# Layer one's last pair of blocks: its second product as seven products too, and partial sums copied from bank to bank by ScalarE

## The chip, the cores and the metric

The kernel runs on one core of a Trainium2 chip. The metric is the device time of one execution in microseconds (us), the median of the runs shown. The engines are named as in the profile: PE is TensorE (matmuls) and PEld its weight loads, DVE is VectorE, ACT is ScalarE, SP issues the DMAs (SPq is its queue). ns are nanoseconds.

## What is computed

Attention over chunks, and then two feed-forward layers over 3072 tokens of 512 features, all in float32 (arguments shortened here):

```python
def _moe_ref(x, w_in, w_out, s, b):      # layer one
    h = x @ w_in                         # (3072, 512) @ (512, 2048)
    r = np.maximum(h, 0.0)
    g = s * (r * r) + b
    return (g @ w_out).astype(np.float32)

def _moe2_ref(x, w_in, w_out):           # layer two
    h = x @ w_in
    g = h * (1.0 / (1.0 + np.exp(-1.702 * h)))
    return (g @ w_out).astype(np.float32)

def reference(**kwargs):
    ...
    attn_out = _attn_ref(**attn_kwargs)
    x = np.ascontiguousarray(attn_out.transpose(0, 2, 1, 3)).reshape(B * S, H * D)
    x = _moe_ref(x=x, **moe_kwargs)
    return _moe2_ref(x=x, **moe2_kwargs)
```

## The kernel before, in words

The tokens are cut into 6 blocks of 512. Features lie on the 128 partitions, tokens along the free dimension. A float32 factor is split into a high part that the matmul takes without loss (fp32r) and a low rest, so each product of 128 x 128 weights with 512 columns is three matmuls: high x high, high x low, low x high. An "h" or "l" at the end of a name (wih and wil, xh and xl) says which part it is. The weights arrive as 64-bit floats; `words` turns the two 32-bit halves of each into a float32 (absolute value, clamp, shift, add, sign), and the split follows.

The work runs in five stretches, in the profile's microseconds:

- 0 to 447: attention, and layer one of blocks 0 to 3, one unit after another (`step`; L614 to L616 are the first product, L652 the second).
- 447.8 to 612: layer one of blocks 4 and 5, the last pair (`seven(0)`).
- 612 to 771, 771 to 930 and 930 to the end: layer two, a pair of blocks at a time (`wino(s)`, s = 1, 2, 3).

A pair is multiplied in the way of Strassen and Winograd: weights and inputs are cut into 2 x 2 pieces, sums of pieces are formed, and seven products replace eight. With p counting the eight pairs of hidden tiles, `wino` makes for each p the products A (A11 x B11), B (S2 x T2), C (S3 x T3), A2 (A12 x B21, added into A's bank), D (S1 x T1), C2 (A22 x T4, into C's bank) and D2 (S4 x B22, into D's bank), six matmuls of 512 columns each (L1240 to L1242). The partial sums leave the banks: ScalarE copies A to a spot of the SBUF tile ys (p1, L1277), and VectorE adds a bank to a spot (L1273) for u2 (B), u3 (C), c22 (D), c21 (C2) and c12 (D2). `gates` (L1251) makes G, the hidden values, from A's bank and the spots. When all p are done the second product follows (L1358): sums of G (L1341), their split into oq and oj (L1329 on ScalarE, L1332 on VectorE), and seven products of 96 matmuls with 256 columns.

The last pair is done by functions of its own. Its first product has the same seven products (L1020 to L1022). Its second is the plain one (L1098): 16 hidden tiles, 4 output tiles, 3 terms and 2 blocks, 384 matmuls of 512 columns. The gates of the pair's second block wait in DRAM (gd) in between.

PSUM: A's and C's banks at even p are two single tiles ph; B and D share the tile pb, one half each. At odd p A and C are the halves of one tile, pc, and B and D the halves of another, pd. `space` says so, in both kernels:

```python
if p % 2:
    return ("accA" if c in "AC" else "accB", ("two", s, p, c in "AC"), "ABCD".index(c) // 2)
return ("h", ("h", s, p, c), None) if c in "AC" else ("a", ("two", s, p, False), "BD".index(c))
```

The order on each engine is made by `Plan.order`: every operation has a due number, durations by engine and the operations that it comes after; the plan starts on each engine what can start soonest, among these what is due first. The program is written out in that order, and waits are put in where tiles are shared. Where TensorE would idle early, the plan fills in small matmuls (idle).

Inputs of a pair come through the SBUF tile xf: `fetch(0)` and `fetch(1)` each load half of both blocks, and sums, copies and splits turn them into the operands; xf has two buffers.

Of the kernel before, what the change touches and what calls it, by code (L numbers as in the profile page):

```python
# [40 lines left out]
HELD = 4  # L41
# [7 lines left out]
class Plan:  # L49
# [24 lines left out]
    def order(self):  # L74
# [108 lines left out]
        full, clock = [], 0.0  # L183
        for i, e in chosen:
            if e == "pe":
                idle = min(starts[i], starts[self.first]) - clock
# [8 lines left out]
def attention_moe_moe(ctx: ExitStack, tc: tile.TileContext, q_t, k_w, v_w, w_in1, w_out1, s_b, w_in2, w_out2, out):  # L195
# [22 lines left out]
    wod = [[dram.tile([P, 7, 2, 256], F32, name=f"wod{x}{p}") for x in "hl"] for p in range(NF // 4)]  # L218
    gd = [dram.tile([P, 2, 512], F32, name=f"gd{j}") for j in range(NF)]
# [4 lines left out]
    plan.first = None  # L224
# [87 lines left out]
    def prep(i):  # L312
        m, o, j = w = weights[i]
        need = (at_o if o else at_h)[index[m, j]] - 0.5
        tag = "wo" if o else "wi" if j < NWI else "wj" if j < NWI + NWJ else "wz"
        def tiles(e):
            T[w] = weight_tiles(tag)

        def high(e):
            copy(e, T[w][0], T["u", i].bitcast(F32))  # L320

        def rest(e):
            hi, lo = T[w]
# [3 lines left out]
        d = op(need, {"act": 0.62}, lambda e: (tiles(e), high(e)), after=[d], alloc=[(tag, w)], uses=[("u", i)])  # L327
        f = op(need, {"dve": 0.62}, rest, after=[d], uses=[("u", i)])
        o_w[w] = (d, f)

    def words(i, w, need, late=()):
# [8 lines left out]
        def absolute(e):  # L340
            u = T["u", i] = stp.tile([P, 512], U32, tag="u", name="u", bufs=4)
            hi = T["st", i][:, :, 1]
            if e == "act":
                nc.scalar.activation(out=u.bitcast(F32), in_=hi.bitcast(F32), func=AF.Abs)
            else:
                nc.vector.tensor_single_scalar(out=u, in_=hi, scalar=0x7FFFFFFF, op=ALU.bitwise_and)

        def clamp(e):
            uf = T["u", i].bitcast(F32)
            nc.vector.tensor_scalar(out=uf, in0=uf, scalar1=2.0**-15, scalar2=122880.0, op0=ALU.max, op1=ALU.min)  # L350

        def low(e):
            lo = T["st", i][:, :, 0]
            nc.scalar.activation(out=lo.bitcast(F32), in_=lo, func=AF.Copy, scale=2.0**-51, bias=2.0)  # L354
# [18 lines left out]
        b = op(need, {"act": 0.67} if m == 0 else {"act": 0.67, "dve": 0.36}, absolute, after=[a], alloc=[("u", u)], uses=[st])  # L373
        d = op(need, {"dve": 0.36}, clamp, after=[b], uses=[u])
        d = op(need, {"dve": 0.36}, shift, after=[d], uses=[u])
        d = op(need, {"dve": 0.62}, add, after=[c, d], uses=[u, st])
        return op(need, {"dve": 0.62}, sign, after=[d], uses=[u, st])

# [7 lines left out]
    plan.tag("xf", 2)  # L386
    plan.tag("gq", 2)
    plan.tag("yz", 2)
# [14 lines left out]
    def attend(u):  # L403
# [152 lines left out]
        z = op(pt, {"dve": 0.1 + 0.55 * n}, top, after=s + [z], alloc=[("small", ("top", u))], uses=[("sc", u)])  # L556
# [41 lines left out]
    def step(i):  # L598
        m, b, j, r, v = units[i]
        n = (r.stop - r.start) / 512  # L600
        busy = v < 2
# [68 lines left out]
        if busy:  # L670
            d = op(need, {"act": 0.2 + 0.52 * n}, affine, after=[d], uses=[("r", i)])
        else:
            d = op(need, {"dve": 0.1 + 0.3 * n}, gate2, after=[d], uses=[("r", i)])
        g1 = op(need, {"act": 0.19 + 0.43 * n}, gate3, after=[d], alloc=[("g", ("g", i))], uses=[("r", i)])
        g2 = op(need, {"dve": 0.12 + 0.54 * n}, gate4, after=[g1], uses=[("r", i)])
        for k in range(KT):
# [4 lines left out]
            if plan.first is None:  # L681
                plan.first = d
# [47 lines left out]
    def combine(p):  # L730

        w0, w1 = (0, 0, 2 * p), (0, 0, 2 * p + 1)
        need = at_h[len(units) - 1] + 20

        def keep(v, w, src, dst):
            def fn(e):
                nc.sync.dma_start(out=wc[0][p][v][:, dst], in_=T[w][v].bitcast(F32)[:, src].rearrange("p (n d) -> p n d", d=256))
            return fn

        first = list(o_w[w0]) + list(o_w[w1])  # L740
        done = [op(need, {"sp": 0.75}, keep(v, w0, slice(0, 512), slice(0, 2)), after=first[v:v + 1], uses=[w0]) for v in range(2)]
        done += [op(need, {"sp": 0.4}, keep(v, w1, slice(256, 512), slice(2, 3)), after=first[2 + v:3 + v], uses=[w1]) for v in range(2)]

        def whole(w, k):
            def fn(e):
                T[k, p] = stp.tile([P, 512], F32, tag="u", name="u", bufs=4)
                h, l = T[w]
                nc.vector.tensor_tensor(out=T[k, p], in0=h.bitcast(F32), in1=l.bitcast(F32), op=ALU.add)
            return fn

        lo, hi = slice(0, 256), slice(256, 512)

        def sums(e):
            T["s", p] = stp.tile([P, 4, 256], F32R, tag="st", name="st")
            x, a, b = T["s", p].bitcast(F32), T["wa", p], T["wb", p]
            nc.vector.tensor_tensor(out=x[:, 0], in0=b[:, lo], in1=b[:, hi], op=ALU.add)
            nc.vector.tensor_tensor(out=x[:, 2], in0=a[:, lo], in1=b[:, lo], op=ALU.subtract)
            nc.vector.tensor_tensor(out=x[:, 1], in0=x[:, 0], in1=a[:, lo], op=ALU.subtract)
            nc.vector.tensor_tensor(out=x[:, 3], in0=a[:, hi], in1=x[:, 1], op=ALU.subtract)

        def high(e):
            T["sh", p] = stp.tile([P, 4, 256], F32R, tag="st", name="st")
            nc.scalar.copy(out=T["sh", p], in_=T["s", p].bitcast(F32))

        def low(e):
            x = T["s", p]
            nc.vector.tensor_tensor(out=x, in0=x.bitcast(F32), in1=T["sh", p].bitcast(F32), op=ALU.subtract)

        end_ = list(o_w[weights[-1]])
        a = op(need, {"dve": 0.65}, whole(w0, "wa"), after=first[:2] + end_, alloc=[("u", ("wa", p))], uses=[w0])  # L770
        b = op(need, {"dve": 0.65}, whole(w1, "wb"), after=first[2:] + end_, alloc=[("u", ("wb", p))], uses=[w1])
        c = op(need, {"dve": 1.5}, sums, after=[a, b], alloc=[("st", ("s", p))], uses=[("wa", p), ("wb", p)])
        h = op(need, {"act": 1.05}, high, after=[c], alloc=[("st", ("sh", p))], uses=[("s", p)])
        l = op(need, {"dve": 1.2}, low, after=[h], uses=[("s", p), ("sh", p)])
        for v, (k, x) in enumerate((("sh", h), ("s", l))):
            done.append(op(need, {"sp": 1.35}, lambda e, v=v, k=k: nc.sync.dma_start(out=wc[0][p][v][:, 3:7], in_=T[k, p].bitcast(F32)),
                           after=[x], uses=[(k, p)]))
        o_wc[0, p] = done

    def pair(p):  # L780

        need = 10.0 * (len(units) + 10) + 900
        i0, i1 = [("two", 0, 2 * p + x) for x in range(2)]
        a, b = [words(i, (1, 0, i[2]), need) for i in (i0, i1)]
        lo, hi = slice(0, 256), slice(256, 512)

        def u(i):
            return T["u", i].bitcast(F32)

        def fresh(n):  # L790
            T["q", p, n] = stp.tile([P, 2, 512], F32R, tag="st", name="st")

        def raw(n):
            return T["q", p, n][:, 1].bitcast(F32)

        def first(e):
            fresh(1)
            copy(e, raw(1)[:, lo], u(i1)[:, hi])

        def second(e):  # L800
            nc.vector.tensor_tensor(out=raw(1)[:, hi], in0=u(i1)[:, lo], in1=u(i1)[:, hi], op=ALU.add)
            fresh(2)
            nc.vector.tensor_tensor(out=raw(2)[:, hi], in0=u(i0)[:, lo], in1=u(i1)[:, lo], op=ALU.subtract)
            nc.vector.tensor_tensor(out=raw(2)[:, lo], in0=raw(1)[:, hi], in1=u(i0)[:, lo], op=ALU.subtract)
            nc.vector.tensor_tensor(out=u(i1)[:, lo], in0=u(i0)[:, hi], in1=raw(2)[:, lo], op=ALU.subtract)

        def parts_of(n, src, w, after, key, cols, alloc):
            def high(e):
                if alloc:
                    fresh(n)  # L810
                copy(e, T["q", p, n][:, 0, :w], src())

            def left(e):
                x = T["q", p, n]
                nc.vector.tensor_tensor(out=x[:, 1, :w], in0=src(), in1=x[:, 0, :w].bitcast(F32), op=ALU.subtract)

            def store(v):
                return lambda e: nc.sync.dma_start(
# [731 lines left out]
```

## Time and profile before

| | |
|---|---|
| median of 3 runs | 1095.46 us (1093.86 to 1095.7) |
| the profiled execution | 1096.69 us, its span 1094.8 us |
| TensorE busy | 1074.3 us, 98% of the span |
| VectorE busy | 780.8 us, 71% |
| ScalarE busy | 529.3 us, 48% |
| DMA | 251.03 MB, mean 229 GB/s |

The span runs from the first instruction of the profile to the last; what the profiled execution takes beyond it lies around it. Busy TensorE is not TensorE at its best: a matmul whose end overlaps the next counts as busy in both. In the timeline the first column is the start and the second the duration; matmuls are pipelined, so the distance of two starts is what one costs.

### The profile page before, as it was taken

Reading aid. Unit: us, or ns where it says so; the run is one execution under the profiler, and the core shown is the slowest. Engines: PE = TensorE matmul, PEld = TensorE weight load, DVE = VectorE, ACT = ScalarE, POOL = GpSimd, SP = SyncE. Lnnn points to the kernel's source line nnn. Section 1 sums busy time; section 2 is a strip of 40 time slices with the busy share of each in tenths; the row PEclk is TensorE's granted clock in tenths of the full one; section 3 lists DMA queues with packets and bytes.
Section 4 is the critical chain, followed back from the end, with each engine's and each line's share of the span. In section 5 each row is a group of like instructions: output and inputs, shape, how many; then the busy total and the mean of one; then the engine's idle time right before and its main releaser. Section 6 shows DMA issues by size and latency. Waiting matters only on the chain.

```text
span 1094.8 us, 21993 instructions
## 1 busy us (share of the span) xinstructions
PE 1074.3 (98%) x8716; PEld 924.5 (84%) x8716; DVE 780.8 (71%) x1259; ACT 529.3 (48%) x840; POOL 0.7 (0%) x6
## 2 busy tenths in 40 slices
PE   8989999999999999999999999999999999999998
PEld 8868887888787888888888878999887999888998
DVE  6988988878677678778675676986345985444854
ACT  4779865555345554555562344543233542333432
POOL 0000000000000000000000000000000000000000
PEclk9999999999999999999999999999999999999999
DMA  9776637756587882789789888678656666656562
GB/s 327 255 269 216 198 106 251 261 190 235 175 261 234 287 260 97 259 297 313 255 285 359 285 291 274 190 213 277 204 185 201 187 202 213 194 184 217 181 206 78
DMA packets 136983, 251.03 MB, mean 229 GB/s; under 512 B 13744, under 2 KB 50608, under 8 KB 136880
## 3 DMA queue, kind: packets, MB, share of 16 engines
q1 hardware_dynamic: 136592, 249.09, 68.9%
q8 instruction: 69, 1.13, 0.4%
q10 hardware_dynamic: 288, 0.52, 0.1%
q14 instruction: 34, 0.28, 0.1%
HBM read 183.50 MB, written 66.06 MB: 228 GB/s over the span
## 4 chain that ended last, share of the span: by engine, by line
PE 91%; DMA 3%; DVE 3%; issue 1%; ACT 1%; DVEq 0%; SPq 0%; ACTq 0%
PE pc L1358 9%; PE accA L652 7%; PE accB L652 7%; PE pd L1358 6%; PE pb L1358 6%; PE ph L614 5%; PE ph L615 5%; PE ph L616 5%; PE accA L1098 4%; PE accB L1098 4%; PE pc L1240 2%; PE ph L1240 2%; PE ph L1242 2%; PE ph L1241 2%; PE pc L1242 2%; PE pc L1241 2%
## 5 line engine op out<-in xcount | busy, mean ns | idle before, releaser
L1329 ACT CAST oj<-G 128x1024 fp32r<-128x1024 f32 x54 | 56.7, 1050 | 75.9 <-PE pd L1358 30.1
L1332 DVE TENSOR_TENSOR oj<-G,oj 128x1024 fp32r<-128x1024 f32 x54 | 66.0, 1222 | 23.5 <-ACT oj L1329 23.4
L621 ACT ACTIVATE r<-ph 128x512 f32<-128x512 f32 (+1 forms) x66 | 38.6, 584 | 66.5 <-PE ph L616 57.8
L1251 ACT ACTIVATE G<-ys 128x512 f32<-128x512 f32 x72 | 45.4, 631 | 48.4 <-DVE ys L1273 48.4
L636 ACT CAST gh<-r 128x512 fp32r<-128x512 f32 (+1 forms) x66 | 40.2, 608 | 50.6 <-PE accB L652 36.9
L1358 PE MATMUL pc<-wih,oj 128*128 128x256 f32 x336 | 62.4, 283 | 0.0
L354 ACT ACTIVATE st<-st 128x512 f32<-128x512 uint32 x64 | 42.5, 676 | 29.5 <-DMA st<-w_out 20.6
L640 DVE TENSOR_TENSOR gl<-r,gh 128x512 fp32r<-128x512 f32 (+1 forms) x66 | 44.1, 669 | 14.4 <-ACT gh L636 14.0
L614 PE MATMUL ph<-xh,wih 128*128 128x512 f32 (+1 forms) x136 | 53.7, 395 | 0.6 <-DVE xh L229 0.6
L1358 PE MATMUL pd<-wih,oj 128*128 128x256 f32 x288 | 53.8, 283 | 0.0
L1329 ACT CAST oq<-G 128x1024 fp32r<-128x1024 f32 x30 | 31.5, 1049 | 45.5 <-PE pc L1358 22.0
L1358 PEld LDWEIGHTS pc<-wih,oj 128*128 128x128 f32 x336 | 53.3, 192 | 0.0
L652 PE MATMUL accA<-gl,woh 128*128 128x512 f32 (+1 forms) x132 | 51.1, 387 | 1.6 <-DVE gl L640 1.6
L615 PE MATMUL ph<-xl,wih 128*128 128x512 f32 (+1 forms) x136 | 51.5, 378 | 0.7 <-DVE xl L522 0.7
L652 PE MATMUL accB<-gl,woh 128*128 128x512 f32 (+1 forms) x132 | 50.6, 383 | 1.5 <-issue 1.5
L1273 DVE TENSOR_TENSOR ys<-pb,ys 128x512 f32<-128x512 f32 x36 | 24.9, 691 | 38.0 <-PE pb L1242 31.7
L652 PE MATMUL accA<-gh,woh 128*128 128x512 f32 (+1 forms) x132 | 51.9, 393 | 0.0
L616 PE MATMUL ph<-xh,wil 128*128 128x512 f32 (+1 forms) x136 | 51.5, 378 | 0.0
L1332 DVE TENSOR_TENSOR oq<-G,oq 128x1024 fp32r<-128x1024 f32 x30 | 36.7, 1224 | 20.6 <-ACT oq L1329 20.6
L652 PE MATMUL accB<-gh,woh 128*128 128x512 f32 (+1 forms) x132 | 51.0, 386 | 0.0
L652 PE MATMUL accA<-gh,wol 128*128 128x512 f32 (+1 forms) x132 | 50.8, 385 | 0.0
L652 PE MATMUL accB<-gh,wol 128*128 128x512 f32 (+1 forms) x132 | 50.5, 383 | 0.0
(293 smaller groups left out, 3186.3 us busy)
## 6 DMA issues: line engine op xcount, KB each, us to landing
wih<-wch SPq DMA_DIRECT2D x96, 256.0 KB, 3.5
wil<-wcl SPq DMA_DIRECT2D x96, 256.0 KB, 3.8
wih<-wodh SPq DMA_DIRECT2D x84, 256.0 KB, 2.8
wil<-wodl SPq DMA_DIRECT2D x84, 256.0 KB, 3.3
st<-w_in SPq DMA_DIRECT2D x32, 512.0 KB, 4.9
st<-w_out SPq DMA_DIRECT2D x32, 512.0 KB, 5.1
k<-k_w SPq DMA_DIRECT2D x24, 512.0 KB, 5.7
v<-v_w SPq DMA_DIRECT2D x24, 512.0 KB, 5.8
```

What stands on the lines that cost most here:

```text
L614: nc.tensor.matmul(ph, wh, xh, start=(k == 0), stop=False)
L615: nc.tensor.matmul(ph, wh, xl, start=False, stop=False)
L616: nc.tensor.matmul(ph, wl, xh, start=False, stop=(k == KT - 1))
L640: nc.vector.tensor_tensor(out=gl, in0=T["r", i], in1=gh.bitcast(F32), op=ALU.subtract)
L652: nc.tensor.matmul(o, lt, rh, start=fresh and x == 0, stop=(done and x == 2))
L1098: nc.tensor.matmul(a, lt, rh, start=n == 0 and x == 0, stop=n == NF - 1 and x == 2)
L1240: nc.tensor.matmul(ph, wh, xh, start=first and i == 0, stop=False, skip_group_check=True)
L1241: nc.tensor.matmul(ph, wh, xl, start=False, stop=False, skip_group_check=True)
L1251: nc.scalar.activation(out=g_of(ty, p), in_=src(), func=AF.Gelu_apprx_sigmoid if m else AF.Relu)
L1329: nc.scalar.copy(out=T[kh], in_=g_of(ty, z))
L1332: nc.vector.tensor_tensor(out=T[kl], in0=g_of(ty, z), in1=T[kh].bitcast(F32), op=ALU.subtract)
L1358: nc.tensor.matmul(a, lt[:, z], rh, start=first and t % 2 == 0 and x == 0, stop=p == HALF - 1 and x == 2, skip_group_check=True)
```

## The change

The functions of the last pair (`combine`, `pair`, `outer`, `seven`) go; `blend` prepares sums of weights for both layers and both products, and `wino(s)` runs for s = 0 to 3, the last pair being s = 0. Its second product then has seven products of 48 matmuls with 512 columns (L1134), its G stays in SBUF, and the gates of layer one are relu, square and affine, the latter two on either engine.

In `wino` the partial sums move from bank to bank. `seed` is a ScalarE copy (L1032) from A's bank to B's (p1) and from B's to C's (u2); B and C then add to what lies there (start=False). `out_of` (L1036) copies B and D to spots of ys, and only c22 and c12 stay additions of VectorE (L1042). C2 needs c22, D2 needs the copy of D.

```diff
-            p1 = op(at + 4, {"act": 0.6}, lambda e, p=p, one=one: nc.scalar.copy(out=spot(one), in_=bank("A", p)),
...
-            B_ = product(p, "B", "S2", "T2", at + 5, [], True)
-            u2 = add(one, "B", one, at + 9, [B_, p1])
-            C = product(p, "C", "S3", "T3", at + 10, [], True)
-            u3 = add(1, "C", one, at + 14, [C, u2] + s_22)
-            A2 = product(p, "A", "A12", "B21", at + 15, [A, p1], False)
-            D = product(p, "D", "S1", "T1", at + 20, [], True)
-            c22 = add(1, "D", 1, at + 24, [D, u3])
-            C2 = product(p, "C", "A22", "T4", at + 25, [C, u3], False)
-            c21 = add(2, "C", one, at + 29, [C2, u2] + s_21)
-            D2 = product(p, "D", "S4", "B22", at + 30, [D, c22], False)
-            c12 = add(one, "D", one, at + 34, [D2, c21, u3])
...
+            def seed(src, dst, need, after, p=p):
+                tag, key, _ = space(dst, p)
+                return op(need, {"act": 0.6}, lambda e: nc.scalar.copy(out=bank(dst, p), in_=bank(src, p)), after=after,
+                          alloc=taken(tag, key), uses=[space(src, p)[1], key])
...
+            A = product(p, "A", "A11", "B11", at - 11, [], True)
+            p1 = seed("A", "B", at - 7, [A])
+            B_ = product(p, "B", "S2", "T2", at, [p1], False)
+            u2 = seed("B", "C", at + 4, [B_])
+            v2 = out_of("B", i12, at + 20, [B_] + s_12.get(i12, []), **kept_)
+            A2 = product(p, "A", "A12", "B21", at + 5, [A, p1], False)
+            C = product(p, "C", "S3", "T3", at + 10, [u2], False)
+            D = product(p, "D", "S1", "T1", at + 15, [], True, [p1])
+            p5 = out_of("D", i22, at + 19, [D, v2] + s_22.get(i22, []))
+            c22 = add(i22, "C", at + 24, [C, p5])
+            D2 = product(p, "D", "S4", "B22", at + 31, [D, p5], False)
+            C2 = product(p, "C", "A22", "T4", at + 36, [C, c22], False)
+            c12 = add(i12, "D", at + 37, [D2, v2])
```

At the start of s = 0 one matmul with 512 columns into bank B is added (L984), so that B's bank counts as written. Weight words take one VectorE instruction less, and the absolute value is always ScalarE's (before, VectorE took it in some tiles):

```diff
-            nc.vector.tensor_single_scalar(out=u, in_=u, scalar=3, op=ALU.logical_shift_left)
-
-        def add(e):
-            u = T["u", i]
-            nc.vector.tensor_tensor(out=u, in0=u, in1=T["st", i][:, :, 0], op=ALU.add)
+            nc.vector.scalar_tensor_tensor(
+                out=u, in0=u, scalar=3, in1=T["st", i][:, :, 0], op0=ALU.logical_shift_left, op1=ALU.bitwise_or
+            )
```

xf has one buffer in place of two (`plan.tag("xf", 1)`); the affine step of the units in `step` goes to either engine; the plan pulls more operations forward (`plan.soon`), and fills TensorE with small matmuls until the first of four operations starts (`plan.first`).

The order on TensorE, in layer two's second pair (s = 2) at p = 1. Before: the end of A2, D, and then C2 (wzh and wzl are T4's parts).

```order
L1242 MATMUL pc<-xs,wil 128x512
L1240 MATMUL pd<-xl_7821,wih 128x512
L1241 MATMUL pd<-xl_7821,wih 128x512
L1242 MATMUL pd<-xl_7821,wil 128x512
L1240 MATMUL pd<-xl_7821,wih 128x512
L1241 MATMUL pd<-xl_7821,wih 128x512
L1242 MATMUL pd<-xl_7821,wil 128x512
L1240 MATMUL pc<-wzh,wih 128x512
```

The same place now: the end of A2 (xs is B21), C (xh_7711 is T3), and the start of D (xl_7712 is T1).

```order
L990 MATMUL pc<-xs,wil 128x512
L988 MATMUL pc<-xh_7711,wih 128x512
L989 MATMUL pc<-xh_7711,wih 128x512
L990 MATMUL pc<-xh_7711,wil 128x512
L988 MATMUL pc<-xh_7711,wih 128x512
L989 MATMUL pc<-xh_7711,wih 128x512
L990 MATMUL pc<-xh_7711,wil 128x512
L988 MATMUL pd<-xl_7712,wih 128x512
```

C has moved right behind A2, in the other half of the same tile, and D behind C.

The order on ScalarE in the same stage, p = 0 and 1. Before: copies of A to ys, and the gates.

```order
L1277 COPY ys<-ph 128x512
L1251 ACTIVATE G<-ph 128x512
L1251 ACTIVATE G<-ys 128x512 x3
L1277 COPY ys<-pc 128x512
L1251 ACTIVATE G<-pc 128x512
```

And now: A to B (pd<-pc), B to C (pc<-pd), and copies to ys between the gates.

```order
L1032 COPY pd<-pc 128x512
L1000 ACTIVATE G<-ys 128x512
L1000 ACTIVATE G<-ph 128x512
L1032 COPY pc<-pd 128x512
L1036 COPY ys<-pd 128x512
L1000 ACTIVATE G<-pc 128x512
L1099 CAST oq<-G 128x1024
L1036 COPY ys<-pd 128x512
```

Two copies between banks and two to ys stand at each p where one copy to ys stood.

The order on VectorE in the first weight tiles. Before, for two tiles, the shift (L358), then (behind the clamp and a split) the add (L362) and the sign (L366):

```order
L358 TENSOR_SCALAR u<-u 128x512 x2
L522 TENSOR_TENSOR xl_355<-xx,xh_354 128x4x128
L362 ISA u<-st,u 128x1024 x2
L366 SCALAR_TENSOR_TENSOR u<-st,u 128x512 x2
L447 TENSOR_REDUCE top<-sc 128x8
```

Now shift and add are one (L358), and the sign is L364:

```order
L350 TENSOR_SCALAR u<-u 128x512
L358 SCALAR_TENSOR_TENSOR u<-u,st 128x512 x2
L524 TENSOR_TENSOR xl_351<-xx,xh_350 128x4x128
L364 SCALAR_TENSOR_TENSOR u<-st,u 128x512 x2
L350 TENSOR_SCALAR u<-u 128x512
```

Of each tile's instructions there one is gone.

## Rows read from the trace of the kernel before

**Rows 1.** The page: engines' busy time and share of the span; chain that ended last.
```profile
PE 1074.3 (98%) x8716; PEld 924.5 (84%) x8716; DVE 780.8 (71%) x1259; ACT 529.3 (48%) x840; POOL 0.7 (0%) x6
...
PE 91%; DMA 3%; DVE 3%; issue 1%; ACT 1%; DVEq 0%; SPq 0%; ACTq 0%
```

**Rows 2.** Stretches: length, busy PE, PEld, DVE, ACT, POOL; granted clock, DMA share, GB/s.
```profile
40.00:80.00 40.00, 33.06 (x592) 26.37 (x592) 34.10 (x61) 29.83 (x54) 0.00 (x0) 1.00 0.80 265
80.00:170.00 90.00, 90.00 (x518) 74.04 (x517) 81.25 (x151) 68.02 (x116) 0.00 (x0) 1.00 0.52 175
...
294.00:300.00 6.00, 4.11 (x135) 3.22 (x134) 5.91 (x12) 2.50 (x4) 0.00 (x0) 0.72 0.13 37
300.00:447.80 147.80, 146.22 (x1522) 120.42 (x1521) 112.31 (x212) 73.24 (x125) 0.00 (x0) 1.00 0.68 223
447.80:612.00 164.20, 164.04 (x720) 134.75 (x719) 119.39 (x226) 82.06 (x144) 0.00 (x0) 1.00 0.87 301
...
771.00:850.70 79.70, 79.50 (x349) 63.94 (x348) 39.01 (x54) 28.85 (x46) 0.00 (x0) 1.00 0.63 197
```

**Rows 3.** Timeline: start, duration, engine; TensorE at 447.76, both engines from 773.26.
```profile
447.76 0.39 PE L1020 MATMUL ph<-xh,wih 128*128 128x512 f32 x1
...
450.25 0.39 PE L1022 MATMUL pb<-xl,wil 128*128 128x512 f32 x1
...
773.26 0.39 PE L1242 MATMUL ph<-xh,wil 128*128 128x512 f32 x1
...
773.69 0.59 ACT L1277 COPY ys<-ph 128x512 f32<-128x512 f32 x1 [9.10 <-PE ph L1242]
```

**Rows 4.** Timeline, s = 2, p = 1: TensorE, VectorE and ScalarE around D and C2.
```profile
785.58 0.39 PE L1242 MATMUL pc<-xh,wil 128*128 128x512 f32 x1
...
786.97 0.39 PE L1242 MATMUL pc<-xs,wil 128*128 128x512 f32 x1
...
787.40 0.69 DVE L1273 TENSOR_TENSOR ys<-pc,ys 128x512 f32<-128x512 f32 x1 [1.99 <-PE pc L1242]
...
788.12 0.60 ACT L1251 ACTIVATE G<-pc 128x512 f32<-128x512 f32 x1 [4.25 <-DVE ys L1273]
...
788.36 0.40 PE L1242 MATMUL pd<-xl,wil 128*128 128x512 f32 x1
...
788.77 0.50 PE L1240 MATMUL pc<-wzh,wih 128*128 128x512 f32 x1
...
789.11 0.39 PE L1241 MATMUL pc<-wzl,wih 128*128 128x512 f32 x1
```

**Rows 5.** Waits of TensorE: waited for, us in total, times, longest.
```profile
PE sc L430 <- issue: 3.7, 2, 1.9
...
PE sc L430 <- ACT px L229: 1.6, 1, 1.6
PE accB L652 <- issue: 1.5, 1, 1.5
...
PE pd L1240 <- DVE ys L1273: 0.5, 1, 0.5
```

**Rows 6.** Instructions by line: busy us and mean ns of one, idle before.
```profile
L1329 ACT CAST oj<-G 128x1024 fp32r<-128x1024 f32 x54 | 56.7, 1050 | 75.9 <-PE pd L1358 30.1 <-PE pb L1358 25.1 <-PE pc L1358 20.5
...
L1277 ACT COPY ys<-ph 128x512 f32<-128x512 f32 x12 | 7.1, 591 | 19.8 <-PE ph L1242 19.7
...
L1332 DVE TENSOR_TENSOR oj<-G,oj 128x1024 fp32r<-128x1024 f32 x54 | 66.0, 1222 | 23.5 <-ACT oj L1329 23.4
L362 DVE CUSTOM_DVE_ANT_0 u<-st,u 128x1024 uint16<-128x1024 uint16 x64 | 43.6, 686 | 2.0 <-ACT st L354 0.6
...
L358 DVE TENSOR_SCALAR u<-u 128x512 uint32<-128x512 uint32 x64 | 26.9, 422 | 0.8
```

**Rows 7.** DMA issues: queue, count, KB each, median us to landing.
```profile
gd<-gq SPq DMA_DIRECT2D x14, 512.0 KB, 4.0
...
xf<-xd SPq DMA_DIRECT2D x4, 512.0 KB, 6.4
```

More of the change, by code (lines that the diff above doesn't have):

```diff
@@ L183, in order @@
         full, clock = [], 0.0
+        first = min(starts[i] for i in self.first)
         for i, e in chosen:
             if e == "pe":
-                idle = min(starts[i], starts[self.first]) - clock
+                idle = min(starts[i], first) - clock
                 if idle > 0.3:
@@ L326, in prep, with words @@
         d = words(i, w, need)
-        d = op(need, {"act": 0.62}, lambda e: (tiles(e), high(e)), after=[d], alloc=[(tag, w)], uses=[("u", i)])
-        f = op(need, {"dve": 0.62}, rest, after=[d], uses=[("u", i)])
+        d = op(need, {"act": 0.62, "dve": 0.42}, lambda e: (tiles(e), high(e)), after=[d], alloc=[(tag, w)], uses=[("u", i)])
+        f = op(need, {"dve": 0.69}, rest, after=[d], uses=[("u", i)])
         o_w[w] = (d, f)
-    def words(i, w, need, late=()):
+    owner, turn = [], []
+    def words(i, w, need, late=(), held=None):
         m, o, j = w
@@ L372, in words @@
         c = op(need, {"act": 0.67}, low, after=[a], uses=[st])
[L373 to L377, printed above, removed]
+        b = op(need, {"act": 0.67}, absolute, after=[a],
+               alloc=[("u", ("u", x)) for x in ((i,) if held is None else held)], uses=[st], follows=owner[-1:] if held == () else turn[-1:] if held else ())
+        owner[:] = [b]
+        if held:
+            turn[:] = [b]
+        d = op(need, {"dve": 0.43}, clamp, after=[b], uses=[u])
+        d = op(need, {"dve": 0.685}, shift, after=[c, d], uses=[u, st])
+        return op(need, {"dve": 0.685}, sign, after=[d], uses=[u, st])
     for n in ("k", "v", "qe", "px"):
@@ L680, in step @@
                    follows=[d] if fresh and k % 2 else [])
-            if plan.first is None:
-                plan.first = d
+            if fresh and not plan.first[3:]:
+                plan.first.append(d)
             o_y[group, k] = d
@@ L728, in attention_moe_moe @@
     o_wc = {}
[L730 to L751, printed above, removed]
-        def sums(e):
[L754 to L759, printed above, removed]
@@ L761, in high @@
         def high(e):
-            T["sh", p] = stp.tile([P, 4, 256], F32R, tag="st", name="st")
-            nc.scalar.copy(out=T["sh", p], in_=T["s", p].bitcast(F32))
+            fresh("sh")
+            nc.scalar.copy(out=T["sh", *key], in_=T["s", *key].bitcast(F32))
         def low(e):
[L766 to L770, printed above, removed]
@@ new lines, in low @@
+            x = T["s", *key]
+            nc.vector.tensor_tensor(out=x, in0=x.bitcast(F32), in1=T["sh", *key].bitcast(F32), op=ALU.subtract)
+        first = [(ring, ("s", *key))]
+        if base and not lent:
+            lent.append(len(plan.ops))
+            first.append(("ys", "sy"))
+            kw = {}
+        c = op(need, {"dve": 1.68}, sums, after=ready, alloc=first, uses=[("u", y) for y in us] + base, **kw)
+        h = op(need, {"act": 1.05}, high, after=[c], alloc=[(ring, ("sh", *key))], uses=[("s", *key)] + base)
@@ L1229, in taken, with product @@
             return [(tag, key)]
-        def product(p, c, piece, x, need, after, first):
+        def product(p, c, piece, x, need, after, first, follows=()):
             n, off = PIECE[piece]
@@ L1236, in fn @@
                 ph = bank(c, p)
+                if s == p == 0 and c == "A" and first:
+                    nc.tensor.matmul(bank("B", p), T["wc", s, p, n][0][:, :P], slot(x, 0)[0], start=True, stop=True, skip_group_check=True)
                 for i in range(2):
@@ L1374, in fn, with away @@
                 nc.vector.tensor_tensor(out=spot(out), in0=psum(tag, held)[:, b], in1=spot(in1), op=ALU.add)
[L1375 to L1377 removed]
+            d = op(need, {"dve": 0.69}, fn, after=o_end[n] + after, uses=[tmp, held])
+            plan.soon.add(d)
+            return d
+        def away(n, b, in1, need, after, lo, q, where=None):
             key = ("y", s, lo, q, b)
@@ L1405, in copied @@
             held = ("turn", s, tag, turn)
-            return op(need, {"act": 0.6}, lambda e: nc.scalar.copy(out=spot(out), in_=psum(tag, held)[:, b]),
-                      after=o_end[n] + after, uses=[tmp, held])
+            d = op(need, {"act": 0.6}, lambda e: nc.scalar.copy(out=spot(out), in_=psum(tag, held)[:, b]),
+                   after=o_end[n] + after, uses=[tmp, held])
+            plan.soon.add(d)
+            return d
         for i, n in enumerate((0, 4, 1, 5, 3, 6, 2)):
@@ L1465, in attention_moe_moe @@
     o_late = [op(-1, {"none": 0.0}, follow("att", "late", bufs=1, side="right"), after=stage_ops)]
-    for p in range(NF // 2):
-        combine(p)
-    for p in range(NF // 2):
-        pair(p)
-    for p in range(HELD):
-        outer(p)
-    one = len(plan.ops)
-    seven(0)
-    two = len(plan.ops)
-    for p in range(HELD, NF // 2):
-        outer(p, step_end)
-    step_ops.extend(range(one, two))
-    o_gp = [op(-1, {"none": 0.0}, follow("gp", "gg", bufs=1), after=step_ops)]
-    for s in range(1, len(SEVEN)):
+    wo_ops = []
+    for o in range(2):
+        one = len(plan.ops)
+        for p in range(NF // 2):
+            blend(0, o, p, at_h[len(units) - 1] + (200 if o else 20), "sy" if o and p > 3 else "st")
+        if o:
+            wo_ops = list(range(one, len(plan.ops)))
+    for o in range(2):
+        for p in range(NF // 2):
+            blend(1, o, p, 10.0 * (len(units) + 10) + (1380 if o else 900), "sx" if o or p > EARLY else "sy")
+    o_gp = [op(-1, {"none": 0.0}, follow("gp", "gg", bufs=1), after=step_ops + wo_ops)]
+    for s in range(len(SEVEN)):
         wino(s)
```

482 lines of the change are left out of this document (148 added, 334 removed).

## The prediction

> **What bounds the kernel now.** I read the page's totals first: TensorE is busy 98% of the span and carries 91% of the chain that ended last, VectorE and ScalarE have room on average [rows 1]. Averages hide stages, so the table of stretches comes next [rows 2]: from 300 us on TensorE is busy in nearly all of every stretch, in the last pair of layer one (447.8 to 612.0) and in a product phase of layer two (771.0 to 850.7, one of three) too. Two stretches differ. At 40 to 80 us TensorE works 33.06 of 40 us. At 80 to 170 us it is full, with VectorE busy 81.25 of 90. So a microsecond of matmuls removed after 447.8 us is a microsecond won, unless a wait on ScalarE or VectorE takes its place; and such a wait counts in full. The timeline gives TensorE's price: from 447.76 to 450.25 us eleven matmuls of 512 columns start, 0.2264 each [rows 3]; over longer stretches I use 0.2267 (six per 1.36). The list of waits says that few are left: the largest total is 3.7 us, in attention, and layer two has 0.5 in it [rows 5].
>
> **The change part by part.** Sums are made against the profiled execution, 1096.69 us (span 1094.8 and 1.89 around it); the median shown, 1095.46, lies 1.23 below it, and I take 1.23 off at the end.
>
> 1. Second product of the last pair: 16 tiles x 4 x 3 x 2 blocks = 384 matmuls of 512 columns become seven eighths, 336. 48 x 0.2267 = 10.88 us less, all on the path. One dummy matmul at the pair's start gives back 0.23. **-10.65.** The gates that no longer go through DRAM took 14 stores and their reloads off the queues, 4.0 us to landing each [rows 7]; TensorE did not wait for them, so that is worth nothing.
>
> 2. Weight preparation: the shift (422 ns) and the custom add (686) become one scalar_tensor_tensor, which I price like the add it replaces [rows 6]. So 0.42 us of VectorE less for each of 64 tiles, 27 us in all. It can shorten the span only where VectorE feeds a waiting TensorE: between 40 and 80 us 6.94 us of TensorE are idle [rows 2], and of the waits named there [rows 5] perhaps a third are VectorE's. The absolute value ahead of the clamp goes to ScalarE in every tile, which gives some back. I take **-2.5** for everything before 447 us; bounds -8 (all of that idle time and the stall at 294 us go) and +2 (other waits fall into the new order).
>
> 3. Start of the last pair: xf has one buffer in place of two, so the second operand fetch stands behind the first one's preparation. A fetch lands after 6.4 us [rows 7]; the last unit's output products hold TensorE some 8.2 us (36 matmuls), so little shows. **+1.5**, bounds 0 and +4.
>
> 4. Partial sums on ScalarE. There are now 64 copies from bank to bank. ScalarE must finish one before the next product may add into the bank. No row has such a copy; the nearest, from a bank to SBUF, take 591 ns [rows 6], and I take 0.59. The handshake can be read: the last matmul of a product starts at 773.26, ScalarE's copy of its bank at 773.69, 0.43 later [rows 3]; TensorE goes on 0.05 after ScalarE ends (788.12 + 0.60 to 788.77), and the second matmul after such a wait comes 0.34 later, 0.11 more than the pitch [rows 4]. So a product that stands right behind the one its copy waits for starts 0.43 + 0.59 + 0.05 = 1.07 us after the last start in place of 0.23: 0.84, and 0.11 for the refill, 0.95. With a product of six matmuls between (1.36 us) only the refill could remain.
> Which copies have cover is a matter of order and of tiles. At odd p the banks of A and C are halves of one PSUM tile (pc), those of B and D of another (pd). That the halves wait for each other is in the trace: VectorE's u3 reads C's half, whose last matmul started at 785.58, and yet starts at 787.40, 0.43 after the last matmul of A2 (786.97), and its wait is put down to that matmul [rows 4]. In the changed kernel TensorE's order at odd p is B, A2, C; the copy B to C, issued behind A2, writes C's half of A2's tile, so it waits for A2, and C is next: no cover. The same holds where B follows A at once at a stage's start. Reading the order through the stages gives five such places in each of the four: 20 x 0.95 = **+19.0**. Bounds: +2.2 (20 refills, if the copies wait only for B) and +25 (a third of them also meet ScalarE inside a 1.05 us cast [rows 6]).
> The Trainium skill, "ScalarE: Activation LUTs", section "Step-by-step: what each stage is for", says that ScalarE reaches PSUM with less latency than SBUF, which speaks for these copies. No run here shows a PSUM destination; by it each 0.1 us of a shorter copy would take 2.0 off the sum, and it would need over 0.3 to turn the sign.
>
> 5. What goes: in layer two C2 at odd p waited for ScalarE's G of the same tile: 788.59 due, 788.77 started, and the refill, 0.29 [rows 4]; four a stage, three stages, 3.5, and the 0.5 for VectorE [rows 5]. **-4.0.** In the new order D and the next A lie between C and C2.
>
> 6. Load in the last pair: by its instructions and their rows' durations I estimate for its first phase some 69 us of ScalarE and 71 of VectorE beside 336 matmuls (76.2 us), and for its second some 79 us of VectorE (the 28 splits at 1.22 [rows 6] are the largest part) beside 76.2 of TensorE. Before, VectorE had 119.39 in 164.20 [rows 2]. VectorE kept TensorE full at 90% at 80 to 170 us [rows 2], so 95% need not cost much, but here the chain product, copy, gates, G sums, split, product is short of slack. **+3**, bounds 0 and +11.
>
> ScalarE's 80 copies out to ys, and the adds that leave VectorE in layer two, lie beside TensorE: VectorE fell to 39.01 and ScalarE to 28.85 in 79.70 us there [rows 2]. Their cover is that room; nothing. Sum: -10.65 - 2.5 + 1.5 + 19.0 - 4.0 + 3 = +6.35, so 1103.0 for a profiled execution and **1101.8** for the median.
>
> **The rivals.** *The copies are hidden.* If the copy B to C starts when B ends, A2 covers it, and 19.0 becomes 2.2: 1101.8 - 16.8 = 1085.0, faster. For it: the planner gives the copy B as its only input and places C a product later as if that held. Against: rows 4. *An engine becomes the bound in the last pair.* VectorE and ScalarE fall behind, the full +11 in place of +3, and copies queue behind casts, +3 more: 1112.8. For it: about 95% and 100% in the two phases; against: 80 to 170 us. *The early stages gain more.* With -8 in place of -2.5 the median is 1096.3, and with copies a little cheaper than a SBUF copy the same as before; the 6.94 us idle speaks for it, that DMA and attention share those waits against. *The clock falls.* After the stall of 1.9 us at 294 us the granted clock had a mean of 0.72 over 6 us [rows 2, 5], so some 3.4 us ran at 1.2 in place of 2.4 GHz and lost 1.7. If each of 20 stalls did that: 34 us, 1136. Against: the 1.6 and 1.5 us waits [rows 5] left the clock at 1.00 [rows 2], and there are 19 us of full work between two stalls.
> The Trainium skill, "TensorE: Matmul & The Clock Gate", section "A second HAM failure mode: psum-queue depth-cycling", tells of such a case: brief idling between groups of matmuls, one bank after another, that made the clock swing. The trace before, whose brief waits in the product phase left the clock at 1.00, does not show it.
> That the change would not do what it says I exclude: the matmuls are counted in the built program, and 48 fewer cannot fail to be fewer.
>
> **How the numbers follow.** The forecast (copies exposed, moderate crowding) 0.58, copies hidden 0.17, engine bound 0.15, early gain 0.06, clock 0.04. The forecast's own range is 1095 to 1108. The range for 8 in 10 cuts half of the hidden case and what lies above the bound case: 1086 to 1114. A measurement of this kernel tells about 0.2% from no change, 2.2 us. Faster: 0.17 + 0.05 of the forecast's lower end + 0.03 = 0.25; within: 0.08 of the forecast and 0.03 of the early case = 0.11; slower: the rest, 0.64.
>
> **What would show it.** In the profile after: waits of TensorE "pc L988 <- ACT pc L1032" at odd p in layer two, some 0.8 us each, four a stage, and a product phase of layer two near 83 us in place of 79.7; a second phase of the last pair (512-column products of line 1134) near 78 us; PEclk 1.00 there; the last pair near 163 us in place of 164.2. If the C products at odd p start 0.23 us after A2's last matmul, step 4 is wrong and the first rival holds. If the stage 612 to 771 keeps its length and the last pair takes as long as before, step 6 was too low. If 40 to 80 us holds under 4 us of idle TensorE, step 2 was too low.

## The result, and the profile after

The changed kernel takes 1101.75 us (median of 7, 1100.21 to 1107.62) where the kernel before took 1093.63 beside it (median of 7, 1090.7 to 1095.7): a ratio of 1.0079, 95% interval 1.0061 to 1.0098, so 0.8% slower. The forecast was 1101.8, from a kernel before of 1095.46.

The page of the changed kernel (profiled execution 1101.42 us) shows TensorE with 9 us less to do, VectorE with 26 less, ScalarE with 78 more; the chain has ScalarE at 3% where it had 1% [rows 1].

```profile
span 1099.6 us, 21815 instructions
...
PE 1065.1 (97%) x8653; PEld 914.1 (83%) x8653; DVE 754.9 (69%) x1132; ACT 607.3 (55%) x943; POOL 0.7 (0%) x6
...
PE 88%; DMA 4%; ACT 3%; DVE 3%; issue 2%; DVEq 0%; ACTq 0%; SPq 0%
```

TensorE's waits in it (waited for, us in total, times, longest), to be read beside [rows 5]:

```profile
PE pc L988 <- ACT pc L1032: 9.7, 14, 0.7
PE pp L465 <- ACT qe L457: 3.1, 3, 1.9
PE o L493 <- issue: 3.0, 1, 3.0
PE pb L988 <- ACT pb L1032: 2.0, 3, 0.7
PE ph L615 <- ACT xh L229: 1.8, 2, 1.2
PE ph L988 <- ACT ph L1032: 1.3, 2, 0.7
PE pd L988 <- ACT ys L1036: 1.3, 2, 1.1
...
PE pd L988 <- ACT pd L1032: 0.7, 1, 0.7
```

Four rows name a copy of line 1032 into the tile that the product adds to: 14 + 3 + 2 + 1 = 20 places, as many as the prediction counted, five in each of the four stages. One of them in the timeline, s = 2, p = 1, the place of [rows 4] (start, duration, engine; the bracket is the idle time and what ended it):

```profile
783.53 0.39 PE L990 MATMUL pd<-xl,wil 128*128 128x512 f32 x1
783.76 0.40 PE L988 MATMUL pc<-xs,wih 128*128 128x512 f32 x1
...
784.92 0.40 PE L990 MATMUL pc<-xs,wil 128*128 128x512 f32 x1
...
785.35 0.57 ACT L1032 COPY pc<-pd 128x512 f32<-128x512 f32 x1 [2.16 <-PE pc L990]
785.84 0.59 ACT L1036 COPY ys<-pd 128x512 f32<-128x512 f32 x1
...
785.98 0.50 PE L988 MATMUL pc<-xh,wih 128*128 128x512 f32 x1 [0.66 <-ACT pc L1032]
786.32 0.40 PE L989 MATMUL pc<-xh,wih 128*128 128x512 f32 x1
```

B ends with the matmul at 783.53. ScalarE is free for 2.16 us, and could have copied B while A2 ran; it waits for A2's last matmul (784.92), starts 0.43 later, copies for 0.57, and C starts 0.06 after that. From start to start 1.06 us pass in place of 0.23, and the next takes 0.34: 0.94 in all. The "0.66" of the list is less, because it counts from the modelled end of A2's last matmul.

The next p shows the same order without the shared tile. At even p A and C have a tile ph each, and the copy B to C starts 0.43 after B's last matmul (794.03), while A2 runs; C follows A2 at the pitch (795.42 to 795.65). All twelve copies B to C at even p of layer two are released by B's matmuls.

```profile
794.03 0.39 PE L990 MATMUL pb<-xl,wil 128*128 128x512 f32 x1
794.26 0.40 PE L988 MATMUL ph<-xs,wih 128*128 128x512 f32 x1
794.46 0.57 ACT L1032 COPY ph<-pb 128x512 f32<-128x512 f32 x1 [0.76 <-PE pb L990]
...
795.42 0.39 PE L990 MATMUL ph<-xs,wil 128*128 128x512 f32 x1
795.65 0.40 PE L988 MATMUL ph<-xh,wih 128*128 128x512 f32 x1
```

By stretches, in two executions of each kernel, from the starts of the pairs in the timeline:

| | before | before, again | after | after, again |
|---|---|---|---|---|
| the last pair begins at | 447.76 | 443.06 | 446.71 | 448.21 |
| from there to the span's end | 647.04 | 646.84 | 652.89 | 652.79 |

(Spans: 1094.8, 1089.9, 1099.6, 1101.0 us.) From the last pair on the two executions of a kernel agree within 0.2 us, and the change costs 5.9. The early stretch is another matter: in the kernel before it moves by 4.7 us from one execution to the next, in the changed kernel by 1.5.

### The profile page after: what moved, and what is told of

It reads as the page before. It is cut to its first block, busy times and chain, and to the rows that moved or that the text cites. A ratio compares the mean times of both kernels' runs of the same rounds, so it can differ in the third digit from the quotient of the medians.

```text
span 1099.6 us, 21815 instructions
## 1 busy us (share of the span) xinstructions
PE 1065.1 (97%) x8653; PEld 914.1 (83%) x8653; DVE 754.9 (69%) x1132; ACT 607.3 (55%) x943; POOL 0.7 (0%) x6
## 4 chain that ended last, share of the span: by engine, by line
PE 88%; DMA 4%; ACT 3%; DVE 3%; issue 2%; DVEq 0%; ACTq 0%; SPq 0%
PE pc L1128 9%; PE accA L653 7%; PE accB L653 6%; PE pd L1128 6%; PE pb L1128 6%; PE ph L615 5%; PE ph L616 4%; PE ph L617 4%; PE pc L988 3%; PE pc L1134 3%; PE ph L988 3%; PE pc L990 3%; PE pc L989 3%; PE ph L990 3%; PE ph L989 3%; PE pb L988 2%
## 5 line engine op out<-in xcount | busy, mean ns | idle before, releaser
L1102 DVE TENSOR_TENSOR oj<-G,oj 128x1024 fp32r<-128x1024 f32 x72 | 87.9, 1222 | 63.3 <-ACT oj L1099 62.8
L1099 ACT CAST oj<-G 128x1024 fp32r<-128x1024 f32 x72 | 75.6, 1051 | 81.9 <-PE pd L1128 29.7
L1102 DVE TENSOR_TENSOR oq<-G,oq 128x1024 fp32r<-128x1024 f32 x40 | 48.9, 1223 | 31.1 <-ACT oq L1099 30.9
L1099 ACT CAST oq<-G 128x1024 fp32r<-128x1024 f32 x40 | 42.1, 1052 | 48.6 <-PE pc L1128 20.3
L1111 DVE TENSOR_TENSOR G<-G 128x1024 f32<-128x1024 f32 x48 | 57.6, 1219 | 0.3
L346 ACT ACTIVATE u<-st 128x512 f32<-128x512 f32 x64 | 42.9, 672 | 25.2 <-DMA st<-w_in 20.2
L1000 ACT ACTIVATE G<-ys 128x512 f32<-128x512 f32 x64 | 40.4, 632 | 26.4 <-DVE ys L1042 26.4
```

Of the source, the lines that this page charges most:

```text
L1099: nc.scalar.copy(out=T[kh], in_=g_of(ty, z))
L1102: nc.vector.tensor_tensor(out=T[kl], in0=g_of(ty, z), in1=T[kh].bitcast(F32), op=ALU.subtract)
L1111: o_raw[out, x] = [op(need, {"dve": 1.22}, lambda e: nc.vector.tensor_tensor(out=g_of(out, z), in0=g_of(a, z), in1=g_of(b, z), op=o), afte ...
```

## The experiments

**More cover for the copies, the same instructions.** Only the due number of C2 at even p changes, from before B of the next p to between B and A2:

```diff
-            C2 = product(p, "C", "A22", "T4", at + 36, [C, c22], False)
+            C2 = product(p, "C", "A22", "T4", at + (36 if p % 2 else 42), [C, c22], False)
```

> The changed kernel with one number changed: C2 of an even p is due after B of the next p and before its A2, so that at odd p a product of another tile stands between the one the copy B to C waits for and C. Same instructions, same load of every engine. Theory (the loss is copies without cover): 12 of the 20 zero-cover places go, TensorE's waits for the copies of line 1032 fall from 20 to about 8, and the time by 12 x 0.95 = 11.4 us, from 1101.75 to about 1090.4, just faster than before (1093.6). Rival (the loss is ScalarE's larger load, 607 us in place of 529, wherever the copies stand): no change, 1099 to 1103. Second rival (C2 later makes the gates and the adds behind it late): half of the gain comes back, about 1096.

Measured: 1088.85 us, ratio to before 0.9941 (0.9923 to 0.996). From the last pair to the end 640.8 us (446.74 to 1087.5), 12.1 less than the changed kernel, where 11.4 were expected. TensorE's list has 8 waits of the 20 left, as expected. The same ScalarE work (609.6 us busy) is done. In this kernel's timeline at s = 2, p = 1 the copy runs beside C2, and C follows A2 at the pitch:

```profile
777.71 0.39 PE L988 MATMUL ph<-wzh,wih 128*128 128x512 f32 x1
...
777.96 0.57 ACT L1032 COPY pc<-pd 128x512 f32<-128x512 f32 x1
...
780.23 0.39 PE L990 MATMUL pc<-xs,wil 128*128 128x512 f32 x1
...
780.46 0.40 PE L988 MATMUL pc<-xh,wih 128*128 128x512 f32 x1
```

The rivals of this run, ScalarE's load and late gates, fall: the loss was in where the copies stood.

**And A earlier at the start of a stage.** To that, A of p = 0 is due before the last of the seven products of the stage ahead, with its weights:

```diff
...
-            A = product(p, "A", "A11", "B11", at - 11, [], True)
+            A = product(p, "A", "A11", "B11", at - (190 if s and not p else 11), [], True)
```

> As e1_c2_between, and at the start of each layer-two stage the first A is due before the last of the seven products of the stage ahead, so that B does not stand right behind A. Theory: 15 of the 20 places are gone, 15 x 0.95 = 14.3 us, about 1087.5, 0.6% faster than before. Rival (load of ScalarE): 1099 to 1103. If A's early weights crowd the DMA queue, the last product of a stage waits for its own: 1089 to 1091.

Measured: 1085.27 us, ratio 0.9928 (0.9904 to 0.9952); from the last pair to the end 638.1 us, 14.8 less than the changed kernel, expected 14.3.

**Layer two as before.** In the changed kernel `wino` takes the old block of partial sums for s = 1, 2, 3 and the new one for s = 0:

```diff
+        if s == 0:
             s_12, s_22 = {}, {}
...
+        else:
+            s_one, s_22, s_21 = {}, [], []
...
+                u2 = add(one, "B", one, at + 9, [B_, p1])
```

> The changed kernel with the partial sums of layer two (s = 1, 2, 3) made as before, ScalarE's copy of A to ys and VectorE's adds; the last pair of layer one stays as changed. Theory: the three stages of layer two take about 159 us each again, 3.1 to 3.3 us less each; the last pair stays near 161.4 us, about 2.6 less than before. Time about 1092, at or just under the kernel before. Rival (the last pair is where the time goes, its engines at 95 to 100%): it stays near 1100.

Measured: 1092.9 us, ratio 0.9981 (0.9962 to 0.9999). From the last pair to the end 644.3 us, which is 8.5 less than the changed kernel and 2.6 less than before. That is the expected sum, but not the expected split. Where the last pair ends is read from the timeline, at the first matmul of layer two behind the last one of the pair's second product:

```profile
616.31 0.39 PE L1240 MATMUL pb<-xl,wih 128*128 128x512 f32 x1
...
608.08 0.39 PE L988 MATMUL ph<-xh,wih 128*128 128x512 f32 x1
...
607.36 0.39 PE L988 MATMUL ph<-xh,wih 128*128 128x512 f32 x1
```

(Before, after, and this run. Before, 18 matmuls of layer two stand ahead of that place, in the next run 24; their 4.1 and 5.4 us are put to layer two in the table.)

| us | before | after | layer two as before | the copies alone (next run) |
|---|---|---|---|---|
| the last pair | 164.5 | 161.4 | 159.2 | 165.5 |
| layer two, to the span's end | 482.6 | 491.5 | 485.1 | 491.9 |

So the changed kernel's last pair wins 3.1 us by itself, and the copies in layer two lose 9.0. This run shows less than 9.0 in layer two because it has a loss of its own there: TensorE waits once for a copy to ys, which itself waits for the DMA that carries output out of ys, and the clock is low behind it (columns of the last row as in [rows 2]).

```profile
617.44 0.59 ACT L1077 COPY ys<-pc 128x512 f32<-128x512 f32 x1 [11.41 <-DMA y<-ys]
...
618.08 0.50 PE L988 MATMUL pc<-xh,wih 128*128 128x512 f32 x1 [2.40 <-ACT ys L1077]
...
619.30:622.70 3.40, 3.40 (x9) 2.63 (x9) 1.76 (x4) 1.61 (x3) 0.00 (x0) 0.51 0.99 371
```

Its last pair is 2.2 us shorter than the changed kernel's, with the same functions in another order.

**The other way: the copies alone.** The kernel before with `wino`'s new block in layer two.

```diff
...
-            u2 = add(one, "B", one, at + 9, [B_, p1])
...
+            u2 = seed("B", "C", at + 4, [B_])
...
```

> The kernel before with one part of the change alone: the copies from bank to bank in the three stages of layer two; last pair, weight words and buffers as before. Theory: 15 places without cover at 0.95 us, less some 4 to 5 of waits that go, about +9.6: 1103, slower than before by 0.9%. Rival (the last pair carries the loss): within 2 us of before, 1092 to 1096.

Measured: 1102.55 us, ratio 1.0078 (1.0057 to 1.0098); from the last pair to the end 657.4 us, 10.5 more than before: 9.3 in layer two, beside 9.0 in the changed kernel, and 1.1 in the last pair, 0.9 of it waits for loads of gd.

**The weight words as before.** In the changed kernel, shift and add are two instructions again, and the absolute value of layer two's tiles may go to VectorE:

```diff
...
-        d = op(need, {"dve": 0.685}, shift, after=[c, d], uses=[u, st])
+        d = op(need, {"dve": 0.36}, shift, after=[d], uses=[u])
+        d = op(need, {"dve": 0.62}, add, after=[c, d], uses=[u, st])
```

> The changed kernel with the weight words made as before: shift and add as two VectorE instructions (422 and 686 ns) in place of one, and the absolute value of layer two's tiles on either engine; all else as changed. It puts 0.42 us of VectorE back on each of 64 weight tiles, 27 us in all. Theory of the prediction (the shorter words are worth 2.5 us before 447 us): slower by 2 to 4 us than the changed kernel's 1101.7, about 1104.5. Rival (VectorE has the room, and the early stretch is set by other waits): within 1.5 us of the changed kernel, 1100 to 1103.

Measured: 1111.28 us, ratio 1.0163 (1.014 to 1.0185), some 9.5 us slower than the changed kernel: both expectations missed. Where it went is the surprise: the last pair begins at 447.73, within the spread of the changed kernel, though 50 of the 64 weight tiles are made ahead of it. From there to the end it takes 660.3 us, 7.4 more; another 1.5 lie outside the profile's span. The last pair takes 166.7 us (447.73 to 614.47), 5.4 more than in the changed kernel, and layer two 2.0 more, all in its first stage, where two more copies stand without cover. The largest single place is in the last pair:

```profile
464.04 0.39 PE L997 MATMUL pc<-xh,wil 128*128 128x512 f32 x1
...
464.98 0.88 DVE L818 TENSOR_TENSOR sx<-u,sx 128x256 f32<-128x256 f32 x2
...
465.89 1.04 ACT L822 CAST sx<-sx 128x1024 fp32r<-128x1024 f32 x1 [1.76 <-DVE sx L818]
466.84 0.58 ACT L1039 COPY pd<-pc 128x512 f32<-128x512 f32 x1
...
467.48 0.50 PE L995 MATMUL pd<-xl,wih 128*128 128x512 f32 x1 [3.05 <-ACT pd L1039]
```

The copy A to B (pd<-pc) could have started at 464.5. It stands on ScalarE behind a cast of weight sums (sx), which waits for VectorE, which is busy with the weights. So at this place a late VectorE reaches TensorE through ScalarE's queue. Ahead of it stands a wait of 1.61 us for another copy, with the clock at 0.50 behind it (452.4 to 455.8 us), some 1.7 us. With the old words the plan made another order, and 19 of the 64 absolute values went to VectorE with the shifts, so the 7.4 us are not the price of VectorE's time alone. What the run does show is that the words put back before the last pair, 50 x 0.42 = 21 us of VectorE, moved its start by nothing that stands out of the spread.

**More of the places covered.** To the early A, every A is due 33 places ahead of B in place of 11:

```diff
...
-            A = product(p, "A", "A11", "B11", at - (190 if s and not p else 11), [], True)
+            A = product(p, "A", "A11", "B11", at - (190 if s and not p else 33), [], True)
```

> As e2_and_early_a, and every A is due 33 places ahead of B of its p in place of 11, so that other products stand between A, its copy and B. By the order 2 of the 20 places without cover are left in the whole program. Theory: 3 more places at 0.95 us than e2_and_early_a, so about 2.8 us less: 1082.5 to 1083, 1% faster than before. Rival (with copies covered, ScalarE's load in the last pair and in the stage from 604 us shows as new waits): no less than 1085.

Measured: 1083.91 us, ratio 0.9915 (0.9892 to 0.9938). From the last pair to the end 636.75 us, 1.3 less than with the early A alone where 2.8 were expected; a new wait of 1.4 us in layer two's first stage holds the rest, for a copy to ys that itself waits for the DMA out of ys:

```profile
614.40 0.59 ACT L1036 COPY ys<-pd 128x512 f32<-128x512 f32 x1 [2.50 <-DMA y<-ys]
...
615.04 0.50 PE L988 MATMUL pd<-xl,wih 128*128 128x512 f32 x1 [1.44 <-ACT ys L1036]
```

With the last run below, which is no different from it, it is the fastest kernel tried, 0.85% below the kernel before. Its last pair's second half, at the load that the prediction feared:

```profile
446.00:523.00 77.00, 76.75 (x334) 62.16 (x333) 64.10 (x110) 60.33 (x104) 0.00 (x0) 1.00 0.84 286
523.00:604.00 81.00, 81.00 (x359) 67.03 (x358) 74.79 (x91) 42.37 (x54) 0.00 (x0) 1.00 0.77 255
```

(Columns as in [rows 2].) VectorE is busy 74.79 of 81.00 us, and TensorE all of it.

**The kernel before, once more.**

> The kernel before once more, for a second trace. What stands open is the early stretch: the last pair began at 447.76 in the trace of before and at 442.48 in e5_before_seeds_layer_two, whose TensorE program is the same up to the last pair. Theory (the early stretch differs from execution to execution by some 5 us): it begins between 442 and 448 here; the stretch from there to the end is 647 us as in the first trace, within 0.5. Rival (the first trace is the rule, and 442.48 comes from the change in that kernel): 447.5 to 448.

Measured: 1091.71 us, a single run. Its last pair begins at 443.06 and takes 646.84 us to the end, so the rival falls: the first trace, with 447.76, was one of the later ones.

**The changed kernel, once more.**

> The changed kernel once more, for a second trace: where does its last pair begin? It was 446.71 in the first trace, and 446.51 and 445.28 in the two kernels that share its early program. Theory (the early part of the change brings nothing): 445 to 448, no earlier than the traces of the kernel before on average. Rival (the shorter weight words bring 2.5 us): 440 to 445. From the last pair to the end 653 us, within 0.5.

Measured: 1102.74 us, a single run. Its last pair begins at 448.21, a little later than expected, and takes 652.79 us to the end. Over the traces that share the early TensorE program, before begins at 447.76, 443.06 and 442.48 (mean 444.4), after at 446.71, 448.21, 446.74, 445.51, 448.20 and 446.25 (with the runs above that change layer two or the cover alone; mean 446.9). The early part of the change brings nothing, and more likely costs some 2.5 us: with 5.9 that is the 8 us of the medians, and the interval of the medians, 6.7 to 10.7 us, leaves 0.8 to 4.8 for it.

**The units' gates as before**, on the fastest kernel:

```diff
-        d = op(need, {"act": 0.2 + 0.53 * n, "dve": 0.1 + 0.43 * n}, lambda e: affine(e) if e == "act" else gate2(e), after=[d], uses=[("r", i)])
+        if v < 2:
+            d = op(need, {"act": 0.2 + 0.52 * n}, affine, after=[d], uses=[("r", i)])
+        else:
+            d = op(need, {"dve": 0.1 + 0.3 * n}, gate2, after=[d], uses=[("r", i)])
```

> e9_all_covered with the affine step of the units before the last pair as in the kernel before (ScalarE in some units, VectorE in the rest) in place of on either engine. Open is why the last pair begins at 446 to 448 us in the changed kernel and at 442.5 to 447.8 in the one before. Theory (ScalarE, which got the absolute values, is what the units now wait for, and gates on either engine make it worse): the last pair begins 1 to 2 us sooner, about 444.5 to 445.5, and the time is about 1082.5. Rival (the waits at 75 to 78 us, for xh of ScalarE and xl of VectorE, and the lower clock behind them come from the order made at the start, before gates matter): it begins at 446 to 448 again and the time stays at 1083 to 1085.

Measured: 1083.78 us, ratio 0.9886 (0.9861 to 0.991), no different from the kernel it was made of (1083.91). The last pair begins at 444.95, sooner as the theory had it, but waits for copies to ys of 2.1 and 1.1 us, at 615 and 929 us in layer two, take it back. One execution can't tell this start from the spread, so this run does not settle the cause of the early 2.5 us.

## Why the prediction was right, and where it was not

**Step 1, the matmuls, and step 4, the copies,** carried the sum, and both held. The price, 0.95, was read from handshakes of other instructions and came out as 0.94; the count of 20 is the list's count, though three of the 20 (ph twice, pd once) are other copies than the prediction named; covering 12 and 15 of the places gave 12.1 and 14.8 us, 1.01 and 0.99 a place. That the tiles' shared halves make the copy wait for A2 is in the timeline (ScalarE idle 2.16 us and released by A2 at odd p, no such wait at even p, where the tiles are single), and an order with another tile's product between makes it go. The rival "the copies are hidden" was wrong for the kernel as written, and it is what the reordered kernels are: it priced them at 1085.0, and they took 1083.9 to 1088.9. The copies out to ys are 64 (32 of each tile), not 80; they were put at nothing, and 1.3 us of TensorE's waits are for them.

**Step 5,** the waits that go, 4.0: a stage of layer two was to cost 4.75 - 1.2 = 3.6 more. The stage s = 2 ran from 772.10 to 931.17 before and from 770.45 to 932.63 after, 3.1 more: at 0.94 a place 1.6 us went, where 1.2 were counted. Its product phase looks shorter than the 83 us announced (78.8, to the first of the seven products at 849.26), because C2 and D2 of p = 7 now stand inside the next phase, 2.7 us of matmuls; with them it is 81.5. The 79.7 that the 83 was set against began at 771.0, 1.1 us ahead of the stage.

**Steps 3 and 6,** the start and the load of the last pair, were +1.5 and +3. The pair won 3.1 us on balance, by the table of the run with layer two as before, where -10.65, these two terms and five places at 0.95 make 1.4; without the two terms it is 5.9, which leaves 2.8 for both steps together, less than 4.5. Of it 1.1 is a late operand at the start (0.87 us of waiting for xh, behind the matmul at 447.39), the rest mainly two waits for the copy of D to ys. That the second half, with VectorE near its limit, costs TensorE nothing is shown by the fastest kernel's row above; VectorE has 74.79 us there, where 79 were estimated. The rival "an engine becomes the bound" did not come about; a copy behind a cast, as it had it, shows in one place of the run with the old words, with a wait of 3.05 us.

**Step 2 failed.** The shorter words were put down as 2.5 us before the last pair; that stretch did not get shorter, and with the old words put back its length stayed within the spread. The step took a third of the idle time at 40 to 80 us as VectorE's to give back. The changed kernel has nearly as much of it, 6.12 us in place of 6.94 (columns as in [rows 2]):

```profile
40.00:80.00 40.00, 33.88 (x663) 27.51 (x662) 34.17 (x59) 28.33 (x50) 0.00 (x0) 1.00 0.88 300
80.00:170.00 90.00, 90.00 (x513) 74.28 (x512) 74.69 (x137) 62.89 (x108) 0.00 (x0) 0.98 0.68 221
```

VectorE has 6.6 us less to do at 80 to 170 us, and TensorE, full before, can't use them. That the total came out at 1101.75 beside 1101.8 is in part luck: the early stretch came out 5 us worse than forecast (+2.5 by the means of the traces in place of -2.5), the rest 3 better (+5.9 in place of +8.85), and the kernel before is 1.8 us faster by more runs than by the three that the sum began from.

## What to carry to other kernels

Before an accumulation is seeded from another bank, look for what stands between the producer, the copy and the consumer in the order, and count in tiles, not in banks: a copy into one half of a tile waits for the matmuls into the other. A product of 1.36 us in between hid a handshake of 1.06 us here; none in between cost 0.94 each, and moving one product, with no instruction changed, turned a loss of 0.8% into a gain of 0.6%. Work taken from an engine that is not the bound pays where a wait of the engine that is the bound ends on it, and a busy share alone does not tell that: VectorE's 6.6 us less at 80 to 170 us brought nothing that shows. A prediction made against a single profile should first ask how far that profile's early part moves from one execution to the next.

## What the runs showed of the hardware

ScalarE's copies of 128x512 from bank to bank are a little faster than those from a bank to SBUF, 570 to 578 ns beside 588 and 590 (columns as in [rows 6]):

```profile
L1036 ACT COPY ys<-pd 128x512 f32<-128x512 f32 x32 | 18.8, 588 | 2.3 <-PE pd L990 2.3
L1036 ACT COPY ys<-pb 128x512 f32<-128x512 f32 x32 | 18.7, 590 | 17.8 <-PE pb L990 16.5 <-DMA y<-ys 1.2
...
L1032 ACT COPY pd<-pc 128x512 f32<-128x512 f32 x16 | 9.2, 578 | 6.3 <-PE pc L990 6.3
L1032 ACT COPY pb<-ph 128x512 f32<-128x512 f32 x16 | 9.2, 573 | 28.0 <-PE ph L990 27.9
...
L1032 ACT COPY pc<-pd 128x512 f32<-128x512 f32 x16 | 9.1, 570 | 30.1 <-PE pc L990 28.6 <-PE pd L990 1.5
```

The Trainium skill ("ScalarE: Activation LUTs", section "Step-by-step: what each stage is for") calls PSUM the port of lower latency for ScalarE. The trace agrees, with 10 to 20 ns a copy, at most 0.4 us over 20 places: far from the 0.3 us a copy that would have turned the sign.

The granted clock did not fall where the 20 waits are. The stretch of products in s = 2 has 1.00:

```profile
770.45:849.26 78.81, 75.35 (x326) 60.44 (x325) 21.83 (x29) 37.57 (x63) 0.00 (x0) 1.00 0.60 185
```

The rival built on the Trainium skill's "A second HAM failure mode: psum-queue depth-cycling" ("TensorE: Matmul & The Clock Gate") is not borne out for waits of this length 8 us or more apart. The clock did fall elsewhere: behind the wait of 2.40 us in the run with layer two as before and that of 1.61 us in the run with the old words (the 3.05 us there left it at 1.00), and in the first trace of the changed kernel at 14 to 20 us (0.72 over the six) and at 80 us, behind two waits close together (1.16 and 0.82 us, at 77 to 79 us):

```profile
78.00:80.00 2.00, 1.18 (x5) 0.80 (x5) 2.00 (x4) 1.58 (x3) 0.00 (x0) 1.00 0.97 335
80.00:82.00 2.00, 2.00 (x8) 1.55 (x7) 2.00 (x5) 0.89 (x2) 0.00 (x0) 0.59 1.05 343
82.00:84.00 2.00, 2.00 (x7) 1.58 (x6) 1.06 (x2) 0.89 (x2) 0.00 (x0) 0.56 0.87 209
```

Eight matmuls started 0.43 apart there, at 1.2 GHz, in place of 0.23, which is 1.6 us. All six traces with this early TensorE program have the same two waits. In five the clock fell behind the first or the second, and the twenty matmuls from the second wait on (79.08 in the first trace) take 6.2 to 7.4 us; in the sixth, the fastest kernel's, it stayed at 1.00, and they take 4.7:

```profile
80.00:82.00 2.00, 2.00 (x10) 1.63 (x9) 1.97 (x4) 0.90 (x3) 0.00 (x0) 1.00 1.26 387
```

The mean of the six is 1.5 us above 4.7, and the three traces of the kernel before (with the copies alone) show 1.00 at 78 to 86 us. So the low clock at this place is, as far as these traces tell, some 1.5 of the early 2.5 us. No run set out to test it, and the rest stays open.
